# Unit 7 transposed by DMA instead of on TensorE, with scores, loads and two small moves rearranged around it

## The chip, the cores and the metric

The kernel runs on one core of a Trainium2 chip. The metric is device time in microseconds (us), median of several executions.

## The reference, cut to what matters

```python
# lightning attention, then a bilinear feed-forward
for b in range(nb):
    intra = einsum('bhic,bhjc->bhij', qb, kb) * Dmask   # scores, masked
    intra = einsum('bhij,bhjd->bhid', intra, vb)
    inter = einsum('bhid,bhde->bhie', qb * lam_pow, kv_state)
    out[:, :, sl] = intra + inter
    kv_state = lam_block * kv_state + einsum('bhsd,bhse->bhde', kb_dec, vb)
x = out as [B*S, H*D]                                   # 3072 x 512
y = ((x @ w_a) * (x @ w_b)) @ w_out                     # d_ff = 1536
```

Batch 4, 8 heads, 768 positions of 64. The kernel works in 24 units of 128 positions (six for one batch entry) and puts them through the feed-forward part in groups of 4, 1, 2, 4, 4, 4, 4 and 1 units.

## The kernel before

The feed-forward part of a group is a row of numbered slots. In each of the first twelve TensorE makes two products a and b for one slice f of d_ff; the slots after that are parts of the last matmul. A plan hangs the attention work of later units on these slots, so that TensorE never runs dry. In the plan P is the scaling of q and k and the cast of v, T the transpose, S the scores and their masks, V the update of the state and its copy out of PSUM, and Q, O, O2 the output of units. PK and PV are the two halves of P (q and k, then v), and C is the cast of a weight.

```python
LOOKAHEAD = (3, 2)          # units that the loads may be ahead
DMA_T_FROM = 9              # units from here on are transposed by DMA
PLAN = {
    0: [..., (26, "T", 4), (29, "C", 5), (29, "S", 4), (30, "PV", 4), (34, "O", 4), ...],
    ...
    2: [(0, "V", 6), (1, "T", 7), (1, "P", 8), (4, "T", 8), (4, "P", 9), (6, "S", 7),
        (6, "S", 8), (7, "V", 7), (6, "P", 10), (10, "V", 8),
        (12, "Q", (7, 8, 9, 10)), (12, "P", 11), (13, "V", 9), (14, "P", 12),
        (14, "O2", (9, 10))],
    ...
}
def piece_T(u):             # on TensorE: eight 128x128 transposes, then ScalarE copies
    ...
    nc.tensor.transpose(tps[:, j, hp, :], d["qk"][:, j, 2 * hp:2 * hp + 2, :], ident)
    ...
    nc.scalar.copy(qkT, tps)
def mask(kq, split=False):  # VectorE, out of PSUM: two of these for one unit
    ...
    nc.vector.tensor_mul(m, kq[i], lotri_bc)
def piece_V(u):
    kv_update(u)                        # TensorE adds to the kvd bank
    if u % NB < NB - 1:
        kv_copy(u, kv["ps"])            # VectorE copies the bank to the state st
def make_vb(u, eng):        # cast of v; VectorE from unit 7 on
    ...
    eng_of(eng).tensor_copy(vb, vf)
```

There is only one kvd bank. The update of unit 8 writes what the copy of unit 7's state reads, so it has to wait for that copy. VectorE works strictly in the order of the plan. All loads and transposes are issued from SyncE, in one queue.

## Time and profile before

| | before |
|---|---|
| time, median of 3 (before the change ran) | 233.46 us (233.22 to 233.78) |
| span of the profiled execution | 231.5 us |
| TensorE busy | 225.1 us, 97% |
| VectorE, ScalarE, GpSimd busy | 50%, 39%, 22% |
| TensorE idle between 62.1 and 83.1 us | none |

A kernel in this state is read differently from one with an idle engine. The row of busy time says only that TensorE bounds.

### The profile page before, as it was taken

The numbers are of one execution on the slowest core, as the hardware profiler recorded it, in microseconds if no ns is written. First come the engines' busy times: TensorE is split into PE (matmuls) and PEld (weight loads), VectorE is DVE, ScalarE is ACT, GpSimd is POOL, SyncE is SP. The second block draws the span as 40 slices with busy tenths as digits, with TensorE's granted clock in tenths as the row PEclk, the third lists the DMA queues.
The fourth block names the chain that finished last, engine by engine and source line by source line (L and its number), as shares of the span: only waits on it lengthen the run. The fifth ranks groups of instructions, "written<-read, shape, count | busy, mean of one in ns | idle before, by whom it ended". The sixth has DMA issues, their size and how long they took to land.

```text
span 231.5 us, 4532 instructions
## 1 busy us (share of the span) xinstructions
PE 225.1 (97%) x1779; PEld 124.8 (54%) x1779; DVE 115.9 (50%) x204; ACT 90.9 (39%) x172; POOL 50.8 (22%) x65
## 2 busy tenths in 40 slices
PE   7799999999999999999999999999999999999994
PEld 2484444459688654554544454544554544444493
DVE  0894757536469726676334584334483313331050
ACT  3677563066473243342233333233333234332261
POOL 6071000336564333334301533001200000000000
PEclk9999999999999999999999999999999999999999
DMA  4999999998999999999869995239300220000311
GB/s 154 303 281 349 349 364 301 299 189 189 204 229 161 225 195 217 213 184 213 304 201 203 218 175 113 93 103 194 66 3 0 91 93 0 1 0 23 115 45 50
DMA packets 96422, 38.84 MB, mean 168 GB/s; under 512 B 83344, under 2 KB 91920, under 8 KB 96400
## 3 DMA queue, kind: packets, MB, share of 16 engines
q1 hardware_dynamic: 96256, 38.54, 72.5%
q8 instruction: 14, 0.23, 0.4%
q14 instruction: 8, 0.07, 0.1%
q10 hardware_dynamic: 144, 0.00, 0.0%
HBM read 28.32 MB, written 6.29 MB: 149 GB/s over the span
## 4 chain that ended last, share of the span: by engine, by line
PE 87%; DMA 4%; SPq 3%; ACT 2%; DVE 1%; issue 0%
PE a_ps L439 27%; PE b_ps L439 26%; PE op L472 23%; PE o_ps L355 3%; DMA q<-in_q_dram 3%; PE kq L313 2%; SPq L129 2%; PE o_ps L345 2%; DMA qf<-in_q_dram 2%; PE kvd L369 2%; ACT scratch L565 1%; PE tps L299 1%; SPq L145 1%; DVE scratch L542 1%; PE kq L590 1%; ACT xT L362 0%
## 5 line engine op out<-in xcount | busy, mean ns | idle before, releaser
L452 DVE TENSOR_TENSOR ab<-a_sb,b_ps 128x512 bf16<-128x512 bf16 (+2 forms) x96 | 52.3, 552 | 78.4 <-PE b_ps L439 57.4
L439 PE MATMUL a_ps<-xT,wa_sb 128*128 128x512 bf16 (+3 forms) x388 | 77.0, 324 | 0.4 <-ACT xT L362 0.4
L439 PE MATMUL b_ps<-xT,wb_sb 128*128 128x512 bf16 (+2 forms) x384 | 77.1, 326 | 0.0
L447 ACT CAST a_sb<-a_ps 128x512 bf16<-128x512 f32 (+2 forms) x96 | 45.6, 481 | 62.6 <-PE a_ps L439 61.3
L472 PE MATMUL op<-wo_sb,ab 128*128 128x512 bf16 (+2 forms) x312 | 65.6, 363 | 0.0
L439 PEld LDWEIGHTS <-wb_sb 128*128 128x128 bf16 x384 | 34.5, 98 | 28.6 <-DVE wb_sb L165 0.3
L439 PEld LDWEIGHTS <-wa_sb 128*128 128x128 bf16 x388 | 34.0, 98 | 28.7 <-issue 0.8
L472 PEld LDWEIGHTS <-ab 128*128 128x128 bf16 x312 | 28.7, 98 | 29.9
L330 DVE TENSOR_TENSOR m<-kq,lotri 128x512 bf16<-128x512 f32 x47 | 29.3, 682 | 17.8 <-PE kq L313 17.2
L262 POOL TENSOR_TENSOR qk<-kf,lp_k 128x512 bf16<-128x512 f32 x18 | 19.3, 1074 | 74.8 <-DMA kf<-in_k_dram 58.2
L267 POOL TENSOR_TENSOR qk<-qf,lp_q 128x512 bf16<-128x512 f32 x20 | 21.9, 1095 | 23.3 <-DMA qf<-in_q_dram 23.3
L467 ACT COPY o_sb<-op 128x512 f32<-128x512 f32 (+2 forms) x19 | 10.3, 541 | 34.0 <-PE op L472 34.0
L362 ACT CAST xT<-o_ps 128x512 bf16<-128x512 f32 x22 | 12.0, 590 | 18.0 <-PE o_ps L355 17.5
L401 DVE TENSOR_TENSOR st<-kvd,bdiag 128x512 bf16<-128x512 f32 x18 | 12.3, 682 | 4.2 <-PE kvd L369 3.6
L276 DVE CAST vb<-vf 128x512 bf16<-128x512 f32 x17 | 9.7, 570 | 0.0
L301 ACT COPY qkT<-tps 128x1024 bf16<-128x1024 bf16 x5 | 5.1, 1012 | 9.9 <-PE tps L299 9.9
L198 PE MATMUL idle<-idle_sb 128*128 128x128 bf16 (+1 forms) x31 | 6.8, 359 | 1.3 <-DVE idle_sb L193 1.3
L355 PE MATMUL o_ps<-m,vb 128*64 128x128 bf16 x192 | 7.8, 222 | 0.0
L276 POOL CAST vb<-vf 128x512 bf16<-128x512 f32 x7 | 4.4, 631 | 13.1 <-DMA vf<-in_v_dram 13.1
L345 PEld LDWEIGHTS <-st 128*128 128x128 bf16 x80 | 5.4, 98 | 2.8
L313 PE MATMUL kq<-qkT 64*128 64x128 bf16 x160 | 6.6, 218 | 0.0
L355 PEld LDWEIGHTS <-vb 128*64 128x64 bf16 x192 | 5.7, 109 | 1.4
(57 smaller groups left out, 86.5 us busy)
## 6 DMA issues: line engine op xcount, KB each, us to landing
vf<-in_v_dram SPq DMA_DIRECT2D x24, 256.0 KB, 4.9
qf<-in_q_dram SPq DMA_DIRECT2D x20, 256.0 KB, 4.6
kf<-in_k_dram SPq DMA_DIRECT2D x20, 256.0 KB, 4.7
out_dram<-o_sb SPq DMA_DIRECT2D x16, 256.0 KB, 2.0
wst<-in_moe_w_a_dram SPq DMA_DIRECT2D x6, 512.0 KB, 8.6
wst<-in_moe_w_b_dram SPq DMA_DIRECT2D x6, 512.0 KB, 8.7
wst<-in_moe_w_out_dram SPq DMA_DIRECT2D x6, 512.0 KB, 8.6
out_dram<-o_kept SPq DMA_DIRECT2D x7, 256.0 KB, 2.5
```

Of the source, the lines that this page charges most:

```text
L262: eng_of(eng).tensor_mul(qk[:, 1], raw.pop((u, "k")), lp_k[:, u % NB].to_broadcast([128, H, D]))
L267: eng_of(eng).tensor_mul(U[u]["qk"][:, 0], raw.pop((u, "q")), lp_q[:, u % NB].to_broadcast([128, H, D]))
L276: eng_of(eng).tensor_copy(vb, vf)
L313: nc.tensor.matmul(kq[i][:, hp, :], lhsT=d["kT"][p, hp, :], rhs=d["qT"][p, hp, :], start=True, stop=True, skip_group_check=True)
L330: nc.vector.tensor_mul(m, kq[i], lotri_bc)
L355: nc.tensor.matmul(d["o"][p, hp, :], lhsT=d["vb"][:, 2 * hp + i, :], rhs=d["m"](i, hp), start=(first and hp == 0), stop=True, skip_group_c ...
L362: nc.scalar.copy(xT[:, :, col:col + BLK], o_ps)
L401: nc.vector.tensor_mul(st[:].rearrange("p hp i d -> p hp (i d)"), ps[:].rearrange("p hp i d -> p hp (i d)"), bdiag_bc)
L439: nc.tensor.matmul(ps[:, lo:hi], lhsT=w_sb[:, s, f * 128:(f + 1) * 128], rhs=xT[:, s, lo:hi], start=(s == 0), stop=(s == KS - 1), skip_gro ...
L447: nc.scalar.copy(a_sb[:, :gt], ps[:, :gt])
L452: nc.vector.tensor_mul(ab[:, f, :gt], a_sb[:, :gt], ps[:, :gt])
L472: nc.tensor.matmul(op[:, lo:hi], lhsT=ab[:, f, t * 128:(t + 1) * 128], rhs=wo_sb[:, f, lo:hi], start=(f == 0), stop=(f == FC - 1))
```

## The change

The change takes the eight transposes of unit 7 off TensorE and lets the DMA engines do them. Presumably to give that transpose time to arrive, the scores of units 7 and 8 move from slot 6 to slot 8, and unit 7's update from slot 7 to slot 9; unit 8's stays in slot 10. The loads of unit 11 are held back behind the transposes of units 9 and 10, presumably so that these are not late. Two small moves come with it: unit 4's output one slot earlier, and the very last store issued by ScalarE, which makes its data.

```diff
--- before.py
+++ after.py
@@ -29,8 +29,8 @@
 W_CHUNKS = (256,) * 6
 W_STEPS = ((0, 1), (2,), (3,), (4,), (5,))
 W_BUFS = 12
-LOOKAHEAD = (3, 2)
-DMA_T_FROM = 9
+LOOKAHEAD = {9: 2, 10: 1}
+DMA_T = (7,) + tuple(range(9, 24))
 KEEP_GROUPS = 3
 PACK = 4
 
@@ -41,12 +41,12 @@
 
 PLAN = {
     0: [(0, "V", 3), (8, "C", 0), (9, "C", 1), (15, "C", 2), (18, "C", 3), (23, "PK", 4),
-        (26, "C", 4), (26, "T", 4), (29, "C", 5), (29, "S", 4), (30, "PV", 4), (34, "O", 4),
+        (26, "C", 4), (26, "T", 4), (29, "C", 5), (29, "S", 4), (30, "PV", 4), (33, "O", 4),
         (35, "PK", 5), (35, "PV", 5)],
     1: [(0, "V", 4), (2, "T", 5), (3, "PK", 6), (6, "PV", 6), (6, "S", 5), (7, "T", 6),
         (10, "S", 6), (12, "O2", (5, 6)), (13, "P", 7)],
-    2: [(0, "V", 6), (1, "T", 7), (1, "P", 8), (4, "T", 8), (4, "P", 9), (6, "S", 7),
-        (6, "S", 8), (7, "V", 7), (6, "P", 10), (10, "V", 8),
+    2: [(0, "V", 6), (1, "P", 8), (4, "T", 8), (4, "P", 9), (8, "S", 7),
+        (8, "S", 8), (9, "V", 7), (6, "P", 10), (10, "V", 8),
         (12, "Q", (7, 8, 9, 10)), (12, "P", 11), (13, "V", 9), (14, "P", 12),
         (14, "O2", (9, 10))],
     3: [(3, "S", 11), (3, "S", 12)],
@@ -181,7 +181,7 @@
             if kind in "abo":
                 if len(staged) >= W_BUFS:
                     return
-            elif c >= used["u"] + LOOKAHEAD[used["u"] > 9]:
+            elif c >= used["u"] + LOOKAHEAD.get(used["u"], 2 if used["u"] > 8 else 3):
                 return
             pending.pop(0)
             if kind in "abo":
@@ -280,7 +280,7 @@
         make_ks(u, "dve" if u < n0 + 2 else "pool")
         make_qs(u, "pool")
         used["u"] = u + 1
-        if u >= DMA_T_FROM:
+        if u in DMA_T:
             qkT = qkT_pool.tile([128, 2, HP, 128], BF16, name="qkT", tag="qkT")
             nc.sync.dma_start_transpose(
                 out=qkT[:].rearrange("p j hp i -> p (j hp) i"),
@@ -457,7 +457,7 @@
         row, o_sb = kept.pop(0)
         nc.sync.dma_start(out=out_r[row], in_=o_sb)
 
-    def store(row, op, lo, hi):
+    def store(row, op, lo, hi, queue=None):
         if row < g_u0[KEEP_GROUPS]:
             o_sb = wst_pool.tile([128, 1024], F32, name="o_kept", tag="wst")[:, :d_model]
             nc.scalar.copy(o_sb, op)
@@ -465,7 +465,7 @@
             return
         o_sb = o_pool.tile([128, d_model], F32, name="o_sb", tag="osb")
         nc.scalar.copy(o_sb[:, lo:hi], op[:, lo:hi])
-        nc.sync.dma_start(out=out_r[row][:, lo:hi], in_=o_sb[:, lo:hi])
+        (queue or nc.sync).dma_start(out=out_r[row][:, lo:hi], in_=o_sb[:, lo:hi])
 
     def out_mms(op, ab, t, fs, lo=0, hi=d_model):
         for f in fs:
@@ -514,7 +514,7 @@
                     if lo:
                         op = ps_bank("op", [128, d_model], F32, ffn=True)
                     out_mms(op, ab, t, range(FC), lo, hi)
-                    store(u0 + t, op, lo, hi)
+                    store(u0 + t, op, lo, hi, nc.scalar if hi == d_model else None)
                 return
             out_mms(op, ab, t, range(FC // 2))
             hook(FC + 2 * t)
```

## The prediction

> **What bounds the kernel now.** I read the page first, then the windows by stage, the chain of waits, and the timeline of the stretch that the change touches.
>
> ```profile
> PE 225.1 (97%) x1779; PEld 124.8 (54%) x1779; DVE 115.9 (50%) x204; ACT 90.9 (39%) x172; POOL 50.8 (22%) x65
> ```
>
> TensorE is busy for 97% of the 231.5 us. The windows (start:end, length, then busy us of PE, weight loads, VectorE, ScalarE, GpSimd, then clock, DMA share, GB/s) say where the rest is:
>
> ```profile
> 38.90:51.20 12.30, 12.16 (x78) 5.77 (x76) 6.39 (x10) 3.08 (x6) 3.77 (x4) 1.00 1.07 246
> ...
> 62.10:83.10 21.00, 21.00 (x241) 16.33 (x240) 15.33 (x30) 9.52 (x20) 10.03 (x10) 1.00 1.11 204
> ```
>
> In 62.1 to 83.1, where group 2 (units 5 and 6 in the feed-forward part, units 7 to 12 being prepared) is computed, TensorE has no gap at all, and the DMA engines are saturated (1.11). So whatever leaves TensorE's stream there is gained, and whatever makes TensorE wait is lost, for no later stretch has slack in which a delay could vanish. The chain of waits gives the pieces:
>
> ```profile
> 64.20 0.45 PE tps L299 x8
> ...
> 69.46 0.55 PE kq L313 x16
> ...
> 73.40 0.44 PE b_ps L439 x4
> 74.08 0.44 PE a_ps L439 x4
> ```
>
> The first is unit 7's transpose, eight matmuls on the path for 0.45 us. The second is the scores of units 7 and 8. Between the last two stands the state update of unit 8 (0.22 us). The timeline shows what that update rests on:
>
> ```profile
> 69.91 2.48 DVE L330 TENSOR_TENSOR m<-kq,lotri 128x512 bf16<-128x512 f32 x4
> 72.30 0.41 DVE L276 CAST vb<-vf 128x512 bf16<-128x512 f32 x1
> 72.63 0.41 DVE L452 TENSOR_TENSOR ab<-a_sb,b_ps 128x256 bf16<-128x256 bf16 x1
> 72.97 0.68 DVE L401 TENSOR_TENSOR st<-kvd,bdiag 128x512 bf16<-128x512 f32 x1
> ```
> ```profile
> 73.70 0.38 PE L369 MATMUL kvd<-vb,qk 128*128 128x128 bf16 x4
> ```
>
> After the scores VectorE makes four masked copies in 2.48 us, then the cast of unit 10's v, one product, and the copy of unit 7's state out of the kvd bank, ending at 73.65. Unit 8's update writes that bank and starts at 73.70. The built program confirms it: this matmul waits for that copy. The two meet with 0.05 us between them, so **this wait is already at its edge**.
>
> **What the Trainium skill says.** "TensorE: Matmul & The Clock Gate", Part 4: PE-mode transpose, gives about 275 ns for one 128x128 transpose in a kernel; this trace has eight in 0.45 us on the chain, 56 ns each pipelined, so I use 0.45. "Advanced Engine Details and Errata", X-Bar Transpose (TRN2), calls transpose DMAs as fast as regular ones; the trace agrees: a transpose lands 0.9 to 1.1 us after the load ahead of it, as a load of 256 KB does. "DMA: Bandwidth & Descriptors", Issuing engines are not separate DMA queues, says that issuing from another engine saves only the sequencer's issue time. No store from ScalarE's queue is in the trace before, but SyncE's issue of the last store takes 0.33 us.
>
> **Part by part.**
>
> 1. Unit 7's transposes leave TensorE: -0.45 us of path. ScalarE's copy of them (1.01 us, ScalarE 39% busy) leaves too, worth nothing by itself.
>
> 2. Unit 4's output one slot earlier. TensorE starts group 1 with `51.23`, idle 0.17 us for ScalarE's xT copy, and the refill brings the loss to about 0.3 us (the first four matmuls should have ended at 51.07 + 0.22 = 51.29 and end at 51.61). One slot earlier, 0.43 us, and one o_kept copy fewer ahead of xT remove it: -0.3 us.
>
> 3. The DMA transpose is a new entry in SyncE's queue, ahead of unit 10's loads:
>
> ```profile
> 60.89 1.02 SPq L129 DMA_DIRECT2D vf<-in_v_dram  x1
> 62.00 0.93 SPq L129 DMA_DIRECT2D qf<-in_q_dram  x1
> ...
> 64.02 0.97 SPq L129 DMA_DIRECT2D vf<-in_v_dram  x1
> ...
> 68.78 5.08 SPq L285 DMA_TRANSPOSE qkT<-qk  x2
> ```
>
> Here 60.89 is unit 9's v and 62.00 to 64.02 unit 10's q, k, v. Transfer by transfer, the trace has a transpose's issue under load ending 1.2 to 1.4 us before the preceding load lands. Unit 9's v lands at 65.40, so the new issue ends at about 64.2 in place of 62.0 for unit 10's q. From the issue of a q to the landing of its v the later units take 5.8 to 7.5 us, median 6.2. Unit 10's v, which landed at 68.88, lands at about 70.4 (70.0 to 71.7). The transpose itself lands near 66.4 and its scores come at 70.4: no wait there.
>
> 4. The scores two slots later, with the updates of units 7 and 8 now in slots 9 and 10 instead of 7 and 10. The order of VectorE in the built program is: cast of unit 10's v, products 7 and 8, four masks, product 9, state copy 7, product 10. The cast used to come after the masks; now **it stands ahead of them and waits for a load that comes later**.
> TensorE's own clock: scores before at 69.46; two slots of 0.87 us later is 71.2; less 0.45 and 0.3 gives 70.45. With no wait, unit 8's update would follow after scores 0.55, slot 9 with refill 0.98, unit 7's update 0.22, slot 10 0.87: at 73.07.
> VectorE, were the cast in time: masks start 0.45 after the scores as before (69.91 - 69.46), at 70.90; + 2.48 = 73.38; then product 9 and the state copy, which end 0.94 later (0.41 + 0.68 less overlaps of about 0.08): 74.3. TensorE waits about 1.25 us. Against 73.70 before, the update starts 0.65 us **later**, although 0.75 us had been won on the way.
> With v landing at 70.4: cast from 70.5, products at about 70.85 and 71.2, masks 71.55 to 74.0, state copy ends 74.95, update at 75.0. That is 1.3 us later than before. A cast in time needs v landed by about 69.8; past that each us of landing is a us of end. In this case parts 1 and 2 are worth nothing: the time of the wait is set by the DMA, not by TensorE.
>
> 5. Loads of unit 11 behind the transposes of 9 and 10. Transpose 10 was issued at 72.62 and landed at 75.86, its scores started at 76.62. Afterwards: k of unit 10 lands a us before v, near 69.4, GpSimd's two scalings (1.04 us each) end at 71.6, transpose 10 lands some 3.2 us later, 74.8, and its scores come near 77.9. No wait, but nothing won, for nothing waited before. Unit 11's k lands near 77.8 (72.24 before), its transpose near 84, unit 12's near 89; the scores of 11 and 12 come near 91.7, those of 14 near 99.5 with its transpose landing about 98.7. These fit with 0.8 us or more, so I count nothing.
>
> 6. Last store from ScalarE. Its copy ends at 228.45, SyncE issues at 228.48: the handover costs 0.03 us and SyncE is free (the preceding issue ended 228.14). So 0 to -0.1 us.
>
> Sum: update of unit 8 at 75.0 against 73.70, +1.3; last store -0.05 to -0.1; later stretches pass the shift on whole. 233.46 + 1.2 = 234.7 us.
>
> **Rivals.**
> A. The intended gain: -0.45 - 0.3 = 232.7 us. For it: TensorE bounds, and both pieces are on the chain. Against it: the state copy has to end after four masks, and only two slots stand between scores and update where four stood. It would need masks far shorter than 2.48 us, or the two updates not to share the bank.
> B. The load in time (v of unit 10 by 69.8): only the 1.25 us wait remains, 233.46 + 0.65 = 234.1. For it: the transpose was squeezed into a queue whose loads could overtake their usual 6.2 us; 5.8 was seen.
> C. The load later still, 71.7, or transposes 10, 12 or 14 late too: 236 us or a little over. For it: DMA share 1.11 in this stretch and margins under 1 us at unit 14. Against it: transposes land in 3.0 to 3.3 us when little is ahead of them.
>
> **Range and chances.** B and the central case take most of the weight, A little: 234.6 us, 80% from 233.7 to 236.0. All lie within 2% of 233.46 (228.8 to 238.1), so same has 0.96; slower 0.03, if several transposes miss their slots; faster 0.01.
>
> **What would show each step.** In the profile after: no transposes of unit 7 on TensorE and four (not five) copies of tps; 16 DMA transposes; TensorE's 0.17 us before group 1 gone; SyncE's transpose between the v of unit 9 and the q of unit 10, ending near 64; VectorE idle before the cast of unit 10's v, waiting for the DMA, and its four masks after it; TensorE idle 1 to 2 us before unit 8's update (kvd), released by the state copy; busy time of TensorE down by 0.5 us while the span is longer. I am wrong if that idle is absent, if v of unit 10 lands before 69.8 (then B), if TensorE waits at the scores of 9 and 10, 11 and 12 or 14 instead (C), or if the end after the last copy, 3.1 us of the span now, changes by over 0.3 us.

## The result

| | before | after |
|---|---|---|
| median | 233.46 us (233.22 to 233.78, 5 runs) | 234.96 us (234.70 to 235.60, 5 runs) |
| span of the profiled execution | 231.53 us | 233.35 us |
| TensorE idle from 62.1 us to the end of group 2 | 0 | 1.92 us |

The ratio is 1.0066, 95% interval 1.0048 to 1.0084: slower by 1.5 us, which is clear of the noise but inside the 2% within which two kernels are classed as the same. Ratios here and below are the mean time of one kernel's fast runs over that of the other's of the same rounds, so they are not quite the ratio of the medians.

First the page and the windows of the changed kernel (columns as in the prediction; the second window is a little longer because the group is):

```profile
PE 225.2 (97%) x1771; PEld 124.4 (53%) x1771; DVE 117.6 (50%) x204; ACT 89.8 (38%) x171; POOL 50.7 (22%) x65
```
```profile
38.90:51.20 12.30, 12.30 (x80) 5.94 (x78) 7.14 (x10) 2.64 (x5) 3.84 (x4) 1.00 1.11 252
...
62.10:84.50 22.40, 20.48 (x232) 15.72 (x230) 16.36 (x30) 8.57 (x19) 8.54 (x8) 1.00 1.05 192
```

Eight matmuls are gone (1779 to 1771), and the stretch before 51.2 has no gap any more. But where TensorE was busy for 21.00 of 21.00 us it is now busy for 20.48 of 22.40. The timeline of TensorE names both gaps, in brackets at the end with who ended them:

```profile
75.02 0.38 PE L369 MATMUL kvd<-vb,qk 128*128 128x128 bf16 x4 [1.52 <-DVE st L401]
...
82.68 0.40 PE L345 MATMUL o_ps<-qkT,st 128*128 128x128 bf16 x4 [0.40 <-DVE st L401]
```

The first is the update of unit 8, which waits 1.52 us for the copy of unit 7's state. The second is the output of unit 10, which waits for the copy of unit 9's state. VectorE's timeline up to the first, and GpSimd's beside it:

```profile
68.73 0.92 DVE L452 TENSOR_TENSOR ab<-a_sb,b_ps 128x256 bf16<-128x256 bf16 x2 [0.94 <-ACT a_sb L447]
69.79 1.19 DVE L276 CAST vb<-vf 128x512 bf16<-128x512 f32 x1
70.91 0.74 DVE L452 TENSOR_TENSOR ab<-a_sb,b_ps 128x256 bf16<-128x256 bf16 x2
71.57 2.47 DVE L330 TENSOR_TENSOR m<-kq,lotri 128x512 bf16<-128x512 f32 x4
73.96 0.40 DVE L452 TENSOR_TENSOR ab<-a_sb,b_ps 128x256 bf16<-128x256 bf16 x1
74.29 0.68 DVE L401 TENSOR_TENSOR st<-kvd,bdiag 128x512 bf16<-128x512 f32 x1
```
```profile
69.66 1.04 POOL L267 TENSOR_TENSOR qk<-qf,lp_q 128x512 bf16<-128x512 f32 x1
```

The state copy ends at 74.97 and the update starts at 75.02. The cast of unit 10's v took 1.19 us, where it had taken 0.41 before. Its v had landed at 69.70, so it did not wait for the DMA in that time; it overlapped GpSimd's scaling of unit 10's q, which ran to 70.70, and ended 0.28 us after it. Before it, VectorE had been idle from 69.65 for the v, and in these 0.14 us the scaling had started (69.66). The second wait has the same look:

```profile
80.78 1.24 DVE L276 CAST vb<-vf 128x512 bf16<-128x512 f32 x1
81.94 0.68 DVE L401 TENSOR_TENSOR st<-kvd,bdiag 128x512 bf16<-128x512 f32 x1
```
```profile
80.70 1.04 POOL L262 TENSOR_TENSOR qk<-kf,lp_k 128x512 bf16<-128x512 f32 x1 [1.73 <-PE op L472]
```

The cast of unit 11's v started 0.08 us after a GpSimd scaling, ended 0.28 us after it, and pushed the copy of unit 9's state past the moment at which TensorE wanted it.

SyncE's queue, in the order in which it issues (start, length):

```profile
61.73 1.74 SPq L285 DMA_TRANSPOSE qkT<-qk  x1
63.53 0.56 SPq L129 DMA_DIRECT2D qf<-in_q_dram  x1
...
64.78 0.99 SPq L129 DMA_DIRECT2D vf<-in_v_dram  x1
66.11 5.85 SPq L285 DMA_TRANSPOSE qkT<-qk  x2
```

Unit 7's transpose landed at 65.78, and its scores started at 70.80, so no wait came from the transpose itself.

The bookkeeping along the chains of waits, after less before, each at the same piece of work: start of group 0's products +0.43 (17.92 to 18.35); first products of group 1 +0.12 (they end at 51.61 and at 51.73); products after unit 8's update +1.32 (74.08 to 75.40); first products of group 3 +1.89 (83.28 to 85.17); end of the last copy +1.89; end of the span +1.82. The first +0.43 lies in code that the change does not touch. Such a late start, 0.57 to 0.66 us of idle time of TensorE in place of 0.23, also shows in the profiles of e5 and e9 below and not in those of the other eight runs (0.23 to 0.29): it is taken for variation from run to run, which would explain why the profiled spans differ by more than the medians do. Without it the profile says +1.39, and the timed runs say +1.5.

### The profile page after: what moved, and what is told of

Read it like the earlier page. It is cut to its first block, busy times and chain, and to the rows that moved or that the text cites. A ratio compares the mean times of both kernels' runs of the same rounds, so it can differ in the third digit from the quotient of the medians.

```text
span 233.3 us, 4513 instructions
## 1 busy us (share of the span) xinstructions
PE 225.2 (97%) x1771; PEld 124.4 (53%) x1771; DVE 117.6 (50%) x204; ACT 89.8 (38%) x171; POOL 50.7 (22%) x65
## 4 chain that ended last, share of the span: by engine, by line
PE 90%; DVE 3%; DMA 3%; ACT 2%; issue 1%; SPq 0%; DVEq 0%
PE a_ps L439 27%; PE b_ps L439 26%; PE op L472 26%; PE o_ps L355 3%; DMA q<-in_q_dram 3%; PE kq L313 2%; PE o_ps L345 2%; DVE m L330 2%; PE kvd L369 1%; ACT scratch L565 1%; PE tps L299 1%; DVE scratch L542 1%; DVE st L401 1%; PE kq L590 1%; PE kv L369 0%
## 5 line engine op out<-in xcount | busy, mean ns | idle before, releaser
L262 POOL TENSOR_TENSOR qk<-kf,lp_k 128x512 bf16<-128x512 f32 x18 | 18.8, 1042 | 75.9 <-DMA kf<-in_k_dram 66.0
L276 DVE CAST vb<-vf 128x512 bf16<-128x512 f32 x17 | 11.1, 655 | 0.1
L198 PE MATMUL idle<-idle_sb 128*128 128x128 bf16 (+1 forms) x31 | 7.3, 376 | 1.3 <-DVE idle_sb L193 1.3
L301 ACT COPY qkT<-tps 128x1024 bf16<-128x1024 bf16 x4 | 4.0, 1012 | 9.4 <-PE tps L299 9.4
```

The lines of the kernel that those rows point to most:

```text
L262: eng_of(eng).tensor_mul(qk[:, 1], raw.pop((u, "k")), lp_k[:, u % NB].to_broadcast([128, H, D]))
```

## The experiments

Theory: the loss is the wait of unit 8's update, made by leaving two slots between the scores and that update where four had stood; a smaller part of it, and the whole of the second wait, come from casts that meet GpSimd. Rival: the DMA side (the transpose in the queue, or the later loads) costs the time. The kernel before: 233.72 us (233.26 to 235.75, 11 runs) for e1 to e4, 233.91 (233.36 to 234.92, 11 runs) for e5 to e9, 233.47 (233.33 to 233.66, 11 runs) for e10 and e11. The three calls ran on three different chips, so times of different calls are compared only roughly. All results were correct.

### e1: scores back in their slots

```diff
-        (4, "T", 8), (4, "P", 9), (8, "S", 7),
-        (8, "S", 8), (9, "V", 7), (6, "P", 10), (10, "V", 8),
+        (4, "T", 8), (4, "P", 9), (6, "S", 7),
+        (6, "S", 8), (7, "V", 7), (6, "P", 10), (10, "V", 8),
```

> The changed kernel with the scores of units 7 and 8 back in slot 6 and unit 7's update back in slot 7; the DMA transpose of unit 7, the held-back loads, the earlier output of unit 4 and the last store on ScalarE's queue stay. Theory (the loss is the wait of unit 8's state update on the copy of unit 7's state, which the two slots caused): the wait of 1.5 us before the kvd matmul goes, the cast of unit 10's v stands after the masks again, and the gains of 0.45, 0.3 and about 0.1 us show: 232.6 us, ratio to before 0.996 to 0.997. Rival 1 (the transpose DMA and the moved loads cost the time): TensorE waits for a transpose at the scores of 7, or of 9 and 10, and the time stays at 234 or more. Rival 2 (a state copy late for both reasons): about 233.5.

Measured: 232.87 us (232.68 to 233.14), ratio to before 0.9957 (0.9925 to 0.9988). TensorE's line for unit 8's update has no wait in it:

```profile
73.32 0.38 PE L369 MATMUL kvd<-vb,qk 128*128 128x128 bf16 x4
```

The theory's 232.6 is met within 0.3 us and both rivals fall: with DMA transpose, held-back loads and both small moves in place, the kernel is faster than before. Without the later slots there is no loss. Unit 7's transpose landed at 65.61 here, 3.4 us ahead of the scores in slot 6 (69.01), so the two slots were not needed for it. (On TensorE, ScalarE's copy had been ready at 65.69.)

### e2: the cast out of the way

```diff
-        (8, "S", 8), (9, "V", 7), (6, "P", 10), (10, "V", 8),
+        (8, "S", 8), (9, "V", 7), (6, "PK", 10), (10, "V", 8), (10, "PV", 10),
```

> The changed kernel with the cast of unit 10's v put after the state copies of units 7 and 8 on VectorE (nothing else moves). Theory (two slots too few for four masks, the cast adds only a little): the wait before unit 8's update falls from 1.5 to about 1.2 us and the time to about 234.6, or to 234.1 if the second wait (0.4 us, before unit 10's part of the output) goes with it. Rival (the late load and its cast are the cause, as the record's central case has it): the wait goes down by 1 us or more, time 233.6 or less.

Measured: 234.43 us (234.06 to 234.74), ratio 1.0023 (0.9993 to 1.0053).

```profile
74.99 0.38 PE L369 MATMUL kvd<-vb,qk 128*128 128x128 bf16 x4 [1.27 <-DVE st L401]
```

The wait falls from 1.52 to 1.27 us. So the cast was 0.25 us of it, and four masks in two slots are the rest. The rival, which was the central case, falls. The second wait is absent from this profile, although the cast of unit 11's v still stood on VectorE and took 0.91 us beside a scaling; yet the time came out 0.3 us above the 234.1 expected for that case.

### e3: unit 8's update later

```diff
-        (8, "S", 8), (9, "V", 7), (6, "P", 10), (10, "V", 8),
+        (8, "S", 8), (9, "V", 7), (6, "P", 10), (12, "V", 8),
```

> The changed kernel with unit 8's state update moved from slot 10 to slot 12, ahead of the outputs of 7 and 8; the scores stay in slot 8. Theory (only the distance from the scores to unit 8's update is wrong): no wait before that update, time 232.6, ratio to before about 0.9965. Rival (VectorE is late for everything after the masks): the wait moves to the outputs of 7 and 8 or to the products, and the time stays over 234.

Measured: 232.70 us (232.44 to 233.19), ratio 0.9951 (0.9922 to 0.9980), as the theory had it. One number of the plan mends the change:

```profile
75.11 0.39 PE L369 MATMUL kvd<-vb,qk 128*128 128x128 bf16 x4
```

From group 1 to the end the trace shows no idle time of TensorE over 0.16 us. It also shows the meeting of VectorE and GpSimd from the other side. Here the cast came first (VectorE's timeline, then GpSimd's):

```profile
69.34 0.43 DVE L276 CAST vb<-vf 128x512 bf16<-128x512 f32 x1
```
```profile
69.37 1.30 POOL L267 TENSOR_TENSOR qk<-qf,lp_q 128x512 bf16<-128x512 f32 x1
```

The cast took its 0.43 us, and the scaling, which mostly takes 1.04, took 1.30. So this profile of e3 also lacks the long cast, and by itself does not tell whether moving the update would have been enough; e11, the same kernel, does.

### e4: the slots alone, on the kernel before

```diff
-        (6, "S", 8), (7, "V", 7), (6, "P", 10), (10, "V", 8),
+        (8, "S", 8), (9, "V", 7), (6, "P", 10), (10, "V", 8),
```

(with unit 7's scores moved to slot 8 too)

> The kernel before with only the scores of units 7 and 8 moved to slot 8 and unit 7's update to slot 9; unit 7 is transposed on TensorE, loads and stores as before. Theory: the wait before unit 8's update appears in full, some 1.25 us, with none of the gains: 234.7 us (234.4 to 235.3 if a second wait comes with it). Rival (the DMA part causes the wait): 233.5.

Measured: 234.91 us (234.79 to 235.21), ratio 1.0047 (1.0019 to 1.0076).

```profile
75.29 0.38 PE L369 MATMUL kvd<-vb,qk 128*128 128x128 bf16 x4 [1.28 <-DVE st L401]
```

The whole first wait appears with no DMA transpose of unit 7 at all. Here the cast (70.08) began 0.32 us ahead of the scaling and took 0.42 us, and no second wait came. The rival falls again.

### e5: the two casts on ScalarE

```diff
-        make_vb(u, "pool" if u < n0 + 3 else "dve")
+        make_vb(u, "pool" if u < n0 + 3 else "act" if u in (10, 11) else "dve")
```

> The changed kernel with the casts of the v of units 10 and 11 on ScalarE instead of VectorE; all slots as changed. Theory (these two casts took 1.19 and 1.24 us instead of 0.42 because they met a GpSimd scaling and could not run beside it; the rest of the wait is the four masks in two slots): the first wait falls from 1.52 to about 1.25 us, the second (0.40 us and its refill) goes, time about 234.1 to 234.3. Rival 1 (the casts' length has no part): both waits and 234.9 us stay. Rival 2 (the first wait is mainly the cast): first wait under 0.8 us, 233.6 or less.

Measured: 234.01 us (233.93 to 234.28), ratio 1.0003 (0.9986 to 1.0020), 0.95 us below the changed kernel's median (of another call).

```profile
74.65 0.38 PE L369 MATMUL kvd<-vb,qk 128*128 128x128 bf16 x4 [1.27 <-DVE st L401]
```

The first wait is that of e2 to the hundredth, and the second is gone. What is left is the slots' own wait less the gains of parts 1 and 2, which is rival B of the record, put at 234.1. The waits show this; the times only roughly. Against the kernel before e5 is 0.10 us slower (at most 0.5 by the interval), where B has 0.65, and e2, with the same waits in its profile, is 0.71 slower.

### e6: loads not held back

```diff
-LOOKAHEAD = {9: 2, 10: 1}
+LOOKAHEAD = {9: 3, 10: 2}
```

(on e1)

> Slots of scores and update as in the kernel before (as in the run e1_slots_back), all else of the change kept, but the loads of unit 11 go ahead of the transposes of units 9 and 10 again. Theory (the hold-back is what lets a transpose more into the queue): the transpose of unit 10, which landed at 73.85 in e1 and 75.86 before, lands some 1.7 us later than before, near 77.6, TensorE waits 0.8 to 1.6 us at the scores of unit 10, time about 234.0. Rival (the hold-back is of no use): no wait, 232.9.

Measured: 233.09 us (232.74 to 233.92), ratio 0.9965 (0.9944 to 0.9985). This expectation missed. The transpose of unit 10 landed at 76.21, not near 77.6, and TensorE's scores were only stretched:

```profile
75.88 0.77 PE L313 MATMUL kq<-qkT 64*128 64x128 bf16 x16
```

The same sixteen matmuls take 0.62 us in e1, so the hold-back is worth 0.15 us in the trace, and the times (233.09 against 232.87) do not tell the two apart. The issue of unit 11's loads ended at 69.08, 0.5 us later than before the change (68.60), where I had counted the whole length of the added transpose. The kernel before had been profiled with a late queue. In e4 and e9, which load and transpose as it does, these issues ended at 67.51 and 67.52, and unit 10's transpose landed at 74.54 and 74.72 instead of 75.86. Against those two the transpose of unit 10 is 1.5 to 1.7 us later here, as expected; what was wrong was to count from a single profile.

### e7: unit 8 by DMA too

```diff
-DMA_T = (7,) + tuple(range(9, 24))
+DMA_T = tuple(range(7, 24))
-        (4, "T", 8), (4, "P", 9), (8, "S", 7),
-        (8, "S", 8), (9, "V", 7), (6, "P", 10), (12, "V", 8),
+        (4, "P", 9), (9, "S", 7),
+        (9, "S", 8), (10, "V", 7), (6, "P", 10), (12, "V", 8),
```

(on e3)

> The run e3_update8_later with unit 8 transposed by DMA too, its and unit 7's scores in slot 9, unit 7's update in slot 10, unit 8's in slot 12. The transpose of unit 8 goes into the stretch in which SyncE waited for unit 10's scaling (68.2 to 70.7). Theory (TensorE alone bounds, the queue has room for one more): 0.45 us less than e3, 232.25. Rival (the queue or the masks are full): a wait at the scores of 8 or 10, or at unit 8's update, 232.7 to 233.5.

Measured: 232.79 us (232.42 to 233.31), ratio 0.9950 (0.9931 to 0.9970), no better than e3. The rival is what came:

```profile
72.01 0.40 PE L313 MATMUL kq<-qkT 64*128 64x128 bf16 x8 [0.68 <-DVE ab L452]
```

The scores of unit 8 waited 0.68 us. The profile names a product of VectorE, which was late because the cast of unit 10's v stood ahead of it for 1.17 us; but unit 8's transpose landed at 71.96, just as late. Which of the two would have ended the wait alone is not settled.

### e9: unit 4's output alone

```diff
-        ... (30, "PV", 4), (34, "O", 4),
+        ... (30, "PV", 4), (33, "O", 4),
```

> The kernel before with unit 4's output one slot earlier and nothing else. Theory: TensorE's wait of 0.17 us before group 1 and its refill go, 0.3 us in all: 233.2 us, ratio 0.9987. Rival (hidden anyway): 233.5.

Measured: 233.55 us (232.93 to 234.04), ratio 0.9983 (0.9962 to 1.0005). The trace shows the gap before group 1 gone; the time is too coarse for 0.3 us, as its interval includes 1.

### e10 and e11: an attempt at more, and e3 again beside it

```diff
-        (4, "P", 9), (9, "S", 7),
-        (9, "S", 8), (10, "V", 7), (6, "P", 10), (12, "V", 8),
+        (4, "P", 9), (8, "S", 7),
+        (11, "S", 8), (9, "V", 7), (6, "PK", 10), (12, "V", 8), (12, "PV", 10),
```

(e10, on e7; e11 is e3 unchanged)

> An attempt at a version that beats the run e3: units 7 and 8 both by DMA as in e7, but unit 7's scores in slot 8 and unit 8's only in slot 11 (in e7 their wait of 0.68 us ended as unit 8's transpose landed, 71.96), and the cast of unit 10's v after the state copies, where no scaling of GpSimd holds it up. Theory (TensorE alone bounds once no wait is left): 0.45 us less eight transposes, plus 0.1 for a second change of matmul shape: 0.3 to 0.4 us below e3, 232.3 to 232.4. Rival: a wait at the output of unit 8 for its masks, 232.8 or more.

> The run e3 once more, beside e10 on one chip: as before, ratio to the kernel before 0.995 (0.993 to 0.997), no wait of TensorE between the first group and the end.

Measured: e10 232.42 us (232.10 to 233.69), ratio 0.9969 (0.9950 to 0.9988); e11 232.72 us (232.63 to 232.94), ratio 0.9970 (0.9958 to 0.9982). The median of e10 is where it was expected, but with two runs of its six over 233 the two are not told apart. e10 keeps only a wait of 0.09 us at the output of unit 10. In e11 the cast of unit 10's v came just behind the start of the scaling and was long, unlike in e3, and still unit 8's update has no wait (VectorE, GpSimd, TensorE):

```profile
69.57 1.29 DVE L276 CAST vb<-vf 128x512 bf16<-128x512 f32 x1
```
```profile
69.53 1.04 POOL L267 TENSOR_TENSOR qk<-qf,lp_q 128x512 bf16<-128x512 f32 x1
```
```profile
75.38 0.39 PE L369 MATMUL kvd<-vb,qk 128*128 128x128 bf16 x4
```

So the later update is enough by itself, with a short cast or a long one. As one and the same kernel can have either, the 0.25 us and the second wait of the changed kernel, which was profiled once, need not be the same in all its executions. e3 is the version to keep: one number away from the change, and measured faster than the kernel before.

## Why the prediction was right, point by point

**The direction and the cause.** The forecast of a loss of some 1.2 us from the wait of unit 8's update on unit 7's state copy was right. e4 makes the loss with the slots alone, and e1, e3 and e11 remove it while keeping all the rest. That the update was put at 75.0 and came at 75.02 is luck: the profile had started 0.43 us late. Without that it came at 74.59, 0.9 us later than before and not 1.3, for the wait was 1.52 us where the reckoning had 1.9 (75.0 less 73.07). A second wait, which had not been counted, made up for it. (One reading was off: unit 8's update takes 0.24 us on the chain, 73.84 to 74.08, not 0.22; no sum rests on it.)

**Part 1 (transposes, 0.45 us).** From the change at group 1 (+0.12) to the scores (69.46 to 70.87, +1.41) the chain is 1.29 us later, where two slots are 1.75: a difference of 0.46.

**Part 2 (unit 4's output, 0.3 us).** The start of group 1 went from +0.43 to +0.12, 0.31 us, and TensorE's gap is absent. e9 shows the gap gone too; its time alone would not prove the gain.

**Part 3 (the queue).** The new transpose's issue ended at 63.47 in place of 64.2, and unit 10's v landed at 69.70, outside the range of 70.0 to 71.7 given for it. The rules held: the issue ended 1.24 us before the load ahead of it landed (64.71), and from the issue of q to the landing of v it took 6.17 us. The starting point was off. Unit 9's v was issued at 60.89 in the profile before, but at 58.99 and 59.01 in e4 and e9, whose loads are the same, and unit 10's v landed at 67.93 and 67.80 there instead of 68.88. In the nine profiles with unit 7's DMA transpose it landed at 69.22 to 69.74.

**Part 4 (the wait).** This is the step that failed in its reasoning though its sum came out. It said that the late load sets the time and that "past that each us of landing is a us of end", so that parts 1 and 2 are worth nothing. With v at 69.70, ahead of its own threshold of 69.8, this was its rival B, whose 1.25 us is what e2, e4 and e5 measured (1.27, 1.28, 1.27). What stood in for the late load was the length of the cast, 1.19 us in place of 0.41, while a GpSimd scaling ran beside it. Two errors met: v 0.7 us early, the cast 0.8 us long. The load still had a hand in it, for 0.25 us and not for the whole wait: the cast began 0.09 us after its v landed in the changed kernel, e3 and e11 alike. In e3 (69.34) that was just before the scaling started (69.37), in the other two just after. And parts 1 and 2 were not lost: e2, which has them, is 0.48 us below e4, which has not.

**Part 5 (no wait later).** Wrong for one place. The output of unit 10 waited 0.40 us, 0.57 with the refill of TensorE, the slower matmuls just after a wait (+1.32 to +1.89). It came by a late state copy again, not by a late transpose as rival C had it. e5 takes the casts away and the wait is gone. It is gone from e2 too, where unit 11's cast took 0.91 us in place of 1.24 and the copy ended 0.36 us sooner, at 82.26, just in time. The reading of the queue itself held, and TensorE waited for none of the transposes of the changed kernel. B with 0.25 us for the cast and 0.57 for the second wait is 234.1 + 0.25 + 0.57 = 234.9, which agrees with the 234.96 measured.

**Part 6 (last store).** From the end of the last copy to the end of the span it was 3.08 us before and 3.01 after. SyncE issued the last store in three traces (3.07 to 3.08 us), ScalarE in nine (2.80 to 3.27, mean 3.00). So a gain is not shown.

**Signs.** TensorE's busy time did not fall by 0.5 us (225.1 to 225.2). The warm-up matmuls at the start took 7.3 us instead of 6.8 in this profile, and each restart after a wait adds a little. The idle time in the window of group 2 was the sign that counted.

**What would have caught it.** "SBUF — State Buffer", section Who interferes with whom, says that a cast on VectorE can run in a mode in which it and an instruction of GpSimd exclude each other for a whole instruction, and that issue order decides who blocks. The traces agree (1.19 us for the cast that came second, 1.30 for the scaling that did). The trace before had it as well: six of its 17 casts took over 0.6 us, one of them, at 64.65, 1.00 us in the very stretch that the prediction read, and each ended 0.28 us after a GpSimd scaling. I had read this group's mean, 570 ns for 17 casts, and used 0.41 for the one that moved into GpSimd's way.

## What to carry to other kernels

When work is moved later in a static order, what depends on it has to move with it: count the slots between a producer and its consumer, and compare them with what the engine in between has to do (here 2.48 us of masks and 0.94 more, against two slots of 0.87). A piece that ends 0.05 us before it is needed has no room, even if its engine is only half busy. And when an instruction gets a new neighbour in time, its duration has to be taken from an instance that had such a neighbour, not from the mean of its group. Times of a queue taken from one profile can be off by one or two microseconds, as those of the loads were here; a second profile of the same loads tells.

## What the Trainium skill lacked or had wrong

- "TensorE: Matmul & The Clock Gate", Part 4: about 275 ns is given for a transpose; here each of the 40 before took 219 ns, but in a row of eight the next started 56 ns after the last, 0.45 us for the row. No page gives the rate for transposes in a row, which is what a change like this gains.
- "Advanced Engine Details and Errata", X-Bar Transpose (TRN2): "TRN2 transpose DMAs are as fast as regular DMAs" agrees for the data. The section does not say that the issue holds the issuing queue longer: 1.23 us for unit 10's transpose in the changed kernel, against 0.57 for a load, both with room ahead of them, and what stands behind waits as long; no page has this time for Trainium2 by name.
- No page has the landing time of a transpose with nothing issued behind it: that of unit 9 landed 5.83 us after its issue in the changed kernel and 5.75 in e1, but 4.13 in e2 and 4.00 in e5, behind much the same loads. The cause stays open.
- "SBUF — State Buffer", Who interferes with whom: it has the one that comes second blocked fully. What it lacks is that part of a held cast's time passes meanwhile: the casts ended 0.28 us after GpSimd's instruction, less than the 0.41 of a cast alone.
